# Attention and a bilinear FFN in one kernel: reciprocals of the softmax sums taken on 112 partitions, weights rounded in whole tiles and moved on ScalarE's DMA queue, q scaled and squared on ScalarE

## The chip, the cores and the metric

The kernel runs on one core of a Trainium2 chip. A core has five engines that work side by side, each through its own instructions in order: TensorE (PE, matmuls; its weight loads are PEld), VectorE (DVE), ScalarE (ACT), GpSimd (POOL) and SyncE (SP, which here only issues DMAs). The metric is the time of one execution on the device in microseconds (us), median of several.

## The reference

Weights arrive as float64, all else as float32. Cut to what matters:

```python
batch, n_heads, seq, head_dim = (8, 12, 448, 64)
q_n, k_n = (rmsnorm(q, g_q), rmsnorm(k, g_k))        # x / sqrt(mean(x*x) + 1e-6) * g
scores = np.matmul(q_n, k_n.transpose(0, 1, 3, 2)) / np.sqrt(head_dim)
attn = np.exp(scores - np.max(scores, axis=-1, keepdims=True))
attn = attn / (np.sum(attn, axis=-1, keepdims=True) + 1e-09)
x = np.matmul(attn, v)                               # heads side by side: (3584, 768)
out = ((x @ w_a) * (x @ w_b)) @ w_out                # w_a, w_b: (768, 1536), w_out: (1536, 768)
```

## The kernel before

**Attention.** Two heads make a pair; there are 48 pairs, six for each of the eight batch entries. For a pair, q and k are squared and summed by rows (L418 to L431), the reciprocal root comes from a power on POOL (L441), q is normalized (L445), both are transposed on PE (L474) and copied out of PSUM (`qkT`, L479 to L483). Scores `sc` (L496) come in four chunks of 112 keys; ACT takes the exponential (`ET`, L502, with k's norm as the scale); PE multiplies by v (`o`, L517) and by ones (`su`, L552), which gives each query's sum over keys, the same number on 64 partitions for each head. For the first 12 pairs (`LEAD`) `su` adds the four `ET` chunks on PE itself; later, DVE and POOL add them first (L530, L532). DVE inverts the sums (L570, two RECIPROCALs of 128x224) and multiplies the output by them (L591). In the lead the sums are copied out of PSUM by ACT first (L564) into `sum`, of which there is one buffer; later the RECIPROCAL works in PSUM, in the one buffer `su`.

**Weights.** A float64 weight is rounded to float32 from its two 32-bit words in seven elementwise steps (L260 on ACT, L261 to L267 on DVE, the last add L269 on POOL). Each of the 18 weight tiles comes as two halves of 128x768 that are loaded and rounded apart; four steps (L365, one of them on POOL) then form the further factors that a seven-product (Strassen-like) matrix product needs; the result `st` (7 x 384 columns, three buffers) is stored to DRAM (`kept`) for later use. All DMAs are issued by SP. Words wait in the space of `hT` (`hraw`, the first six weight tiles) and of `fin` (`lraw`).

**FFN.** Two batch entries at a time (`beta` 0 to 3). `quarter_products` makes 12 groups of seven products (`pq`, L741), `last_product` seven products for each of a few row blocks (`po`, L669). Products use two PSUM banks in turn, so DVE and ACT must empty one (L763 to L797) before the product after next. DVE also forms sums of operands (L605, L657).

**Order.** Every operation is entered in `Plan` with an engine, an assumed time, a key, its reads, writes and buffers. `Plan.run` plays the program forward: of the operations that could start soonest on an engine it takes the one with the smallest key. The order of each engine's instructions is what this play gives, and it is fixed when the kernel is built; at run time each engine goes through its list and waits where data are late. Three stretches follow from it: the **lead** (pairs 0 to 11, with the first weight tiles; about 19 to 177 us), the **rounding stage** (FFN of `beta` 0 beside pairs 12 and on, with the rest of the weights; to about 450 us), and the **late stage**.

Of the kernel before, what the change touches and what calls it, by code (L numbers as in the profile page):

```python
# [9 lines left out]
FP32 = mybir.dt.float32  # L10
# [15 lines left out]
class Plan:  # L26
# [6 lines left out]

    TURN = 0.18

# [7 lines left out]
    def op(self, engine, us, key, emit, reads=(), writes=(), new=(), mode=None, chain=None, kb=0):  # L43
# [19 lines left out]
        self.ops.append((engine, us, key, emit, deps, mode, chain, kb, tuple(new), tiles))  # L63
        return n

    def run(self):
# [18 lines left out]
        opened, free, modes, cands, dma = {}, {}, {}, {}, 0.0  # L85
# [25 lines left out]
        while any(cands.values()):  # L111
            best = None
            for e, cs in cands.items():
                f = free.get(e, 0.0) if e else 0.0
                at = {}
                for n in cs:
                    t = buffers(n)
                    if t is not None:
                        turn = self.TURN if ops[n][5] != modes.get(e) else 0.0
                        at[n] = max(f, ready[n], t) + turn  # L120
# [7 lines left out]
            for x in members(n):  # L128
# [14 lines left out]
                for u in users.get(x, ()):  # L143
                    ready[u] = max(ready[u], end[x])
# [15 lines left out]
def kernel(  # L160
# [39 lines left out]
    P = 128  # L200
# [42 lines left out]

    def round_steps(get):
# [7 lines left out]
        def step(do):  # L252
# [16 lines left out]
            ("POOL", 2, step(lambda hi, hif, lo, lof, w, wb: nc.gpsimd.tensor_tensor(w, w, lof, ALU.add)), "x", "w"))  # L269
# [18 lines left out]
    def fast_body(ld, wk, ps_s, ps_o, ps_mm, dram):  # L288
        plan = Plan()
        op, tile_of = plan.op, plan.tile  # L290
        NORM = 4.0
        LEAD = 12

# [5 lines left out]
        def rounding(key, size, get, x, w):  # L299

            for e, n, emit, r, wr in round_steps(get):
                rate = {"ACT": 950, "DVE": 1900 if n == 1 else 950, "POOL": 420}[e]
                op(e, 0.17 + size / rate, key, emit, [{"x": x, "w": w}[c] for c in r], [{"x": x, "w": w}[c] for c in wr])
# [6 lines left out]
        SLOTS, MORE = KO * 2 * S // NW, LATE // NW  # L310
# [5 lines left out]
        op(None, 0.0, -9, open_words, [], [f"{hraw}/{x}" for x in range(SLOTS)] + [f"{lraw}/{x}" for x in range(MORE)],  # L316
           new=[hraw, lraw])

        def place(early):
# [7 lines left out]
            return (lambda: hold[x][:, at * NW:(at + 1) * NW]), f"{name}/{at}"  # L327

        def factors(n, key, early, after):
# [10 lines left out]
            else:  # L340
                m, ab = order[n]
                src = (moe_w_a, moe_w_b)[ab]
                steps = ((0, 4, 3, 2), (1, 5, 0, 3), (0, 3, 4, 0), (0, 6, 1, 3))
            for part, quarters in enumerate((((0, 0), (0, 1)), ((1, 1), (1, 0)))):
                words, row = place(early)

                def load(words=words, quarters=quarters, part=part):
                    if last:
                        k = m + part * MH
                        nc.sync.dma_start(words(), moe_w_out[k * P:(k + 1) * P, :])  # L350
                        return
                    for x, (i, j) in enumerate(quarters):
                        nc.sync.dma_start(
# [632 lines left out]
```

## Time and profile before

| | us |
|---|---|
| median of 3 runs | 1692.31 (1691.57 to 1692.49) |
| the profiled execution | 1693.48 |
| its span, first to last instruction | 1692.0 |
| DVE busy | 891.9 |
| POOL busy | 571.1 |
| ACT busy | 365.9 |

The profile gives for each engine its busy time, a timeline, groups of instructions by source line with their mean duration, and waits: which engine stood idle before which instruction and what ended that. A name such as `pq<-x,st` says what is written and what is read; L741 is a line of the kernel. One float32 matmul of the program stands in the trace as two PE instructions. "PEclk" is the share of its clock that PE was granted.

### The profile page before, as it was taken

To read this page: it belongs to the slowest core of one execution; us is meant where nothing else is said; L and a number is where in the kernel's file an instruction comes from. 1 tells how busy PE (TensorE), PEld (TensorE's weight loads), DVE (VectorE), ACT (ScalarE), POOL (GpSimd) and SP (SyncE) were. 2 spreads that over 40 slices of the span, in tenths; PEclk is the share of its full clock that TensorE was granted. 3 is DMA by queue.
4 is the path that set the end of the run, shared out by engine and by line. 5 is a ranking of instruction groups with operands and counts; after the bars stand their busy time and mean duration, and the time that the engine had idled before them with its cause. 6 is when DMAs were issued, how large, how long until landed. Compare 5 with 4: busy or idle time off the path is not lost.

```text
span 1692.0 us, 14761 instructions
## 1 busy us (share of the span) xinstructions
PE 1606.0 (95%) x5448; PEld 774.1 (46%) x5448; DVE 891.9 (53%) x1094; ACT 365.9 (22%) x654; POOL 571.1 (34%) x326
## 2 busy tenths in 40 slices
PE   5989889988999999999999999999999999999998
PEld 2333334443444444455444544455544455555554
DVE  8996688999766645422265754522236722212331
ACT  5666233211222233200123123200012200000000
POOL 5454456564354444510054355410133200110000
PEclk9999899999999999999999999999999999999999
DMA  6664134444423332321222333222222242222131
GB/s 210 200 200 144 33 119 146 137 170 159 165 83 99 115 123 66 98 98 66 91 81 71 94 98 110 87 98 77 87 72 67 76 168 80 83 98 82 64 112 49
DMA packets 114294, 180.77 MB, mean 107 GB/s; under 512 B 50468, under 2 KB 102948, under 8 KB 104484
## 3 DMA queue, kind: packets, MB, share of 16 engines
q1 hardware_dynamic: 114212, 179.73, 32.0%
q8 instruction: 45, 0.74, 0.2%
q14 instruction: 37, 0.30, 0.1%
HBM read 143.92 MB, written 35.78 MB: 106 GB/s over the span
## 4 chain that ended last, share of the span: by engine, by line
PE 72%; DVE 20%; issue 3%; POOL 3%; DMA 1%; ACT 0%; SPq 0%; DVEq 0%; POOLq 0%; ACTq 0%
PE pq L741 37%; PE po L669 18%; PE sc L496 7%; PE o L517 6%; PE su L552 2%; DVE fin L657 2%; DVE st L261 2%; DVE st L262 2%; DVE st L264 2%; PE pt L474 1%; DVE su L570 1%; DVE sum L570 1%; DVE ms L431 1%; DVE st L365 1%; DVE lraw L267 1%
## 5 line engine op out<-in xcount | busy, mean ns | idle before, releaser
L741 PE MATMUL pq<-x,st 128*128 128x448 f32 x2016 | 780.8, 547 | 29.0 <-DVE U L769 8.6
L741 PEld LDWEIGHTS pq<-x,st 128*128 128x128 f32 x2016 | 383.1, 192 | 414.2 <-issue 373.5
L502 ACT ACTIVATE ET<-sc,ms 112x448 f32<-112x448 f32 x384 | 213.6, 637 | 352.5 <-PE sc L496 334.8
L669 PE MATMUL po<-st,hT 128*128 128x384 f32 x744 | 246.2, 487 | 0.0
L496 PE MATMUL sc<-qkT 64*112 64x448 f32 x768 | 178.4, 582 | 30.3 <-DVE qkT L483 19.5
L669 PEld LDWEIGHTS po<-st,hT 128*128 128x128 f32 x744 | 139.9, 190 | 100.6 <-issue 7.8
L570 DVE RECIPROCAL su<-su 128x224 f32<-128x224 f32 x72 | 112.7, 1565 | 116.9 <-PE su L552 115.8
L517 PE MATMUL o<-ET,v_sb 112*64 112x448 f32 x768 | 169.4, 564 | 3.0 <-ACT x L587 3.0
L532 POOL TENSOR_TENSOR sum<-sum,ET 112x896 f32<-112x896 f32 x72 | 158.8, 2205 | 35.1 <-DVE sum L530 34.1
L441 POOL TENSOR_TENSOR ms<-ms,expo 112x16 f32<-112x16 f32 x48 | 148.3, 3089 | 55.0 <-DVE ms L437 53.4
L788 POOL TENSOR_TENSOR hT<-hT,t 128x448 f32<-128x448 f32 x24 | 28.3, 1180 | 409.6 <-DVE t L787 409.6
L426 POOL TENSOR_TENSOR sq<-k_sb 112x512 f32<-112x512 f32 x36 | 49.4, 1372 | 330.1 <-DMA k_sb<-in_k_dram 205.7
L669 PE MATMUL po<-st,fin 128*128 128x384 f32 x432 | 145.3, 489 | 0.0
L496 PEld LDWEIGHTS sc<-qkT 64*112 64x112 f32 x768 | 62.2, 177 | 126.0 <-issue 68.2
L669 PEld LDWEIGHTS po<-st,fin 128*128 128x128 f32 x432 | 80.6, 190 | 61.2 <-issue 8.8
L517 PEld LDWEIGHTS o<-ET,v_sb 112*64 112x64 f32 x768 | 51.3, 141 | 110.7 <-issue 103.9
L689 DVE TENSOR_TENSOR o_sb<-fin,po 128x384 f32<-128x384 f32 x56 | 31.0, 553 | 110.9 <-PE po L669 110.4
L799 POOL TENSOR_TENSOR hT<-hT,t 128x448 f32<-128x448 f32 x48 | 58.8, 1228 | 61.8 <-DVE t L797 55.5
L763 ACT COPY hT<-pq 128x448 f32<-128x448 f32 x24 | 12.8, 532 | 290.5 <-PE pq L741 290.5
L431 DVE TENSOR_REDUCE ms<-sq 112x8 f32<-112x512 f32 x96 | 65.2, 679 | 13.6 <-POOL sq L426 13.5
L269 POOL TENSOR_TENSOR st<-st,lraw 128x768 f32<-128x768 f32 x24 | 47.5, 1978 | 66.7 <-DVE lraw L267 60.7
L797 DVE TENSOR_TENSOR t<-U,pq 128x448 f32<-128x448 f32 x48 | 29.7, 619 | 67.3 <-PE pq L741 67.3
(70 smaller groups left out, 1120.8 us busy)
## 6 DMA issues: line engine op xcount, KB each, us to landing
st<-kept SPq DMA_DIRECT2D x36, 1344.0 KB, 5.9
st<-kept_o SPq DMA_DIRECT2D x28, 1152.0 KB, 5.2
kept<-st SPq DMA_DIRECT2D x12, 1344.0 KB, 4.6
q_sb<-in_q_dram SPq DMA_DIRECT2D x48, 224.0 KB, 2.8
k_sb<-in_k_dram SPq DMA_DIRECT2D x96, 112.0 KB, 3.0
v_sb<-in_v_dram SPq DMA_DIRECT2D x48, 224.0 KB, 2.6
kept_o<-st SPq DMA_DIRECT2D x6, 1344.0 KB, 6.0
lraw<-in_moe_w_b_dram SPq DMA_DIRECT2D x20, 384.0 KB, 3.5
```

The costliest lines, as they stand in the source:

```text
L269: ("POOL", 2, step(lambda hi, hif, lo, lof, w, wb: nc.gpsimd.tensor_tensor(w, w, lof, ALU.add)), "x", "w"))
L426: nc.gpsimd.tensor_tensor(t, flat, flat, ALU.mult)
L431: nc.vector.tensor_reduce(rs[p][:, s], xs["sq", nm, p], AX, ALU.add)
L441: nc.gpsimd.tensor_tensor(msf, msf, expo, ALU.pow)
L496: nc.tensor.matmul(t[:, e, 0:S], lhsT=qkTs[p][rows, 1, c * SP:(c + 1) * SP], rhs=qkTs[p][rows, 0, :], start=True, stop=True)
L502: nc.scalar.activation(E[:, e], scs[p, c][:, e, 0:S], AF.Exp, scale=rs[p][:, 1, 2 * c + e:2 * c + e + 1])
L517: nc.tensor.matmul(os_[p][e * D:(e + 1) * D, :], lhsT=xs["v", p][:, e, c * D:(c + 1) * D], rhs=ETs[p, c][:, e], start=(c == 0), stop=(c == ...
L532: nc.gpsimd.tensor_tensor(sums[p], sums[p], ETs[p, c], ALU.add)
L570: op("DVE", 1.55, p, lambda half=half: nc.vector.reciprocal(sus[p][:, half], sus[p][:, half]), [], [su])
L669: nc.tensor.matmul(held["po"][:, 0:HALF], lhsT=a[0]()[:, c], rhs=sts[beta, 12 + place_of[f]][:, c], start=(c == 0), stop=(c == MH - 1))
L741: nc.tensor.matmul(banks[bank][:, 0:S], lhsT=sts[at][:, f, c * P:(c + 1) * P], rhs=quads[x][:, c], start=(start and c == 0), stop=(stop an ...
L799: take("POOL", 1.15, lambda i=i, n=n, nm=nm: nc.gpsimd.tensor_tensor(C(i, n), C(i, n), held[nm], ALU.mult), [t], [hp[i]])
```

## The change

- **Sums over keys.** In 44 of the 48 pairs ACT copies the sums out of PSUM (`rec`, three buffers). SP's DMAs spread one row for each head over 56 partitions (`few`, 112x8 for both heads), DVE inverts that, a DMA stores it to DRAM (`inv`), and two DMAs bring it back to 64 partitions each. The last pair of each `beta` (p = 11, 23, 35, 47) is inverted in PSUM as before.
- **Weights.** Each weight tile is rounded as a whole (128x1536), in its seven steps; the last add and all four factor steps are on DVE. Loads and the store to `kept` are issued by ACT.
- **q.** The scale on the way out of PSUM, and the squares of q and k, are on ACT for all pairs.
- **The play.** It counts 0.1 us more where a result goes to another engine (`LAG`), two DMA queues, and lets no operation marked `lock` (of DVE or POOL) start while another one runs. Parts of a quad `x` are tracked one by one. `GATES` and `seq` let eight weight tiles (not six) use the early space.

PE, after the lead. `pt` are transposes, `sc`, `o`, `su` the attention products, `pq` those of the FFN. Before:

```order
L474 MATMUL pt<-ident,k_sb 128x112 x4
L474 MATMUL pt<-ident,qn 128x112 x4
L741 MATMUL pq<-x,st 128x448 x12
L496 MATMUL sc<-qkT 112x448 x4
L517 MATMUL o<-ET,v_sb 64x448 x4
L741 MATMUL pq<-x,st 128x448 x3
L496 MATMUL sc<-qkT 112x448 x4
L552 MATMUL su<-sum,ones 64x448 x2
L517 MATMUL o<-ET,v_sb 64x448 x4
```

The same pair (p = 14) in the changed kernel:

```order
L488 MATMUL pt<-ident,k_sb 128x112 x4
L488 MATMUL pt<-ident,qn 128x112 x4
L776 MATMUL pq<-x,st 128x448 x3
L508 MATMUL sc<-qkT 112x448 x4
L529 MATMUL o<-ET,v_sb 64x448 x4
L776 MATMUL pq<-x,st 128x448 x3
L508 MATMUL sc<-qkT 112x448 x4
L564 MATMUL su<-sum,ones 64x448 x2
L529 MATMUL o<-ET,v_sb 64x448 x4
```

Between two parts of a pair there now stands one FFN product (x3) where there were up to four; most of what is taken out here stands later, as 189 `pq` in one piece.

DVE in the lead, around the reciprocal of a pair (`sum` before, `few` after). Before:

```order
L267 SCALAR_TENSOR_TENSOR hraw<-hraw 128x768
L570 RECIPROCAL sum<-sum 128x224 x2
L365 TENSOR_TENSOR st<-st 128x384 x3
L591 TENSOR_TENSOR x<-x,sum 128x448
L431 TENSOR_REDUCE ms<-sq 112x8
L570 RECIPROCAL sum<-sum 128x224
```

And in the changed kernel:

```order
L600 RECIPROCAL few<-few 112x8
L271 TENSOR_SCALAR st<-st 128x1536
L272 TENSOR_SCALAR st<-st 128x1536
L444 TENSOR_REDUCE ms<-sq 112x8
L451 TENSOR_SCALAR ms<-ms 112x16
L274 SCALAR_TENSOR_TENSOR st<-hraw,st 128x1536
L276 TENSOR_SCALAR hraw<-st 128x1536
L277 SCALAR_TENSOR_TENSOR hraw<-hraw 128x1536
L459 TENSOR_TENSOR qn<-q_sb,ms 112x2x4x64
L626 TENSOR_TENSOR x<-x,rec 128x448
L279 TENSOR_TENSOR st<-st,hraw 128x1536
```

The multiplication by the reciprocal (L626) stands nine rows behind it, and the last add of the rounding (L279) is now a DVE row.

ACT in the lead of the changed kernel, where it issues a load of weights and the store of the weight tile before (before, no DMA stood on ACT):

```order
L495 ACTIVATE qkT<-pt,gain 128x448
L514 ACTIVATE ET<-sc,ms 112x448 x2
L368 DMA hraw<-in_moe_w_b_dram 128x6x256 x2
L386 DMA kept_o<-st 896x1x384
L514 ACTIVATE ET<-sc,ms 112x448 x2
L437 ACTIVATE sq<-k_sb 112x512
L514 ACTIVATE ET<-sc,ms 112x448 x2
L437 ACTIVATE sq<-q_sb 112x512
```

The store waits for DVE's last factor step, and exponentials stand behind it.

The diff, cut to its core:

```diff
-                        at[n] = max(f, ready[n], t) + turn
+                        at[n] = max(f, ready[n], t, port if ops[n][10] else 0.0) + turn
...
+                if ops[x][10]:
+                    port = max(port, t)
                 if ops[x][7]:
-                    dma = max(dma, t) + ops[x][7] / 250.0
-                    end[x] = dma + 2.5
+
+                    dma[e] = max(dma[e], t) + ops[x][7] / (200.0 if dma["SP" if e == "ACT" else "ACT"] > t else 250.0)
+                    end[x] = dma[e] + 2.5
+                    if e == "SP":
+                        dma["ACT"] = max(dma["ACT"], t) + ops[x][7] / 300.0
...
                 for u in users.get(x, ()):
-                    ready[u] = max(ready[u], end[x])
+                    ready[u] = max(ready[u], end[x] + (self.LAG if ops[u][0] != e else 0.0))
...
-            ("POOL", 2, step(lambda hi, hif, lo, lof, w, wb: nc.gpsimd.tensor_tensor(w, w, lof, ALU.add)), "x", "w"))
+            (ROUND, 2, step(lambda hi, hif, lo, lof, w, wb: two[ROUND].tensor_tensor(w, w, lof, ALU.add)), "x", "w"))
...
-        SLOTS, MORE = KO * 2 * S // NW, LATE // NW
+        SLOTS, MORE = KO * 2 * S // (2 * NW), LATE // (2 * NW)
...
+            words, row = place(early)
+
+            for part in range(2):
+                def load(part=part):
+                    to = words()[:, part * NW:(part + 1) * NW]
...
-            parts = [0, 0, 2, 2, 4, 5, 6]
+                        nc.scalar.dma_start(to, moe_w_out[k * P:(k + 1) * P, :])
+                    else:
+                        at = part * HM + m * P
+                        nc.scalar.dma_start(to.rearrange("p (k n) -> p k n", k=KA),
+                                            src[:, 2 * at:2 * (at + P)].rearrange("(k p) n -> p k n", p=P))
+                op("ACT", 0.45, key - 2.5, load, after, [f"{row}/{part}"], kb=768)
...
+                e = FACTOR if pool_ else "DVE"
+                op(e, 1.05 if e == "POOL" else 0.6, key,
...
-            op("SP", 0.5, key, keep, [f"{st}/{x}" for x in range(7)], [f"kept{n}"], kb=1376)
+                    nc.scalar.dma_start(kept[n], sts[n].rearrange("p a b -> p (a b)"))
+            op("ACT", 0.45, key, keep, [f"{st}/{x}" for x in range(7)], [f"kept{n}"], kb=1376)
...
-                op("ACT" if p < LEAD else "POOL", 0.65 if p < LEAD else 1.05, key, square, [f"{nm}{p}"], [sq], new=[sq])
+                e = "ACT" if p < LEAD else SQUARE
+                op(e, {"ACT": 0.65, "POOL": 1.05, "DVE": 0.7}[e], key, square, [f"{nm}{p}"], [sq], new=[sq], lock=e != "ACT")
...
-                    elif p < LEAD:
+                    else:
                         nc.scalar.activation(qkTs[p][:, 0], pts[p, 0][:, 0:S], AF.Copy, scale=gain[:, 0:1])
-                    else:
-                        nc.vector.tensor_scalar_mul(qkTs[p][:, 0], pts[p, 0][:, 0:S], gain[:, 0:1])
...
             if c == 1:
-                op("DVE", 1.12, p, emit, [f"E{p}.0", f"E{p}.1", "moved"], [t], new=[t])
+                op("DVE", 1.12, p, emit, [f"E{p}.0", f"E{p}.1"], [t], new=[t], lock=True)
             else:
-                op("POOL", 2.1, p, emit, [f"E{p}.{c}"], [t])
+                op(ADD_UP, 2.1 if ADD_UP == "POOL" else 1.12, p, emit, [f"E{p}.{c}"], [t], lock=True)
...
+               [f"E{p}.{c}" for c in cs] if p < WIDE else [f"sum{p}"], [su], new=[su] if first else [], mode="cols", chain=chain)
             if not last:
                 return
-            if p < LEAD:
-
-                t = tile_of(f"sum{p}", "sum", 1)
-
-                def move():
-                    x = wk.tile([P, 2, S], FP32, tag="sum", name="sum")[:, 0]
-                    nc.scalar.copy(x, sus[p])
-                    sus[p] = x
-                op("ACT", 0.55, p - 0.5, move, [su], [t, "moved"], new=[t])
-                su = t
-            for x in range(2):
-                half = slice(x * S // 2, (x + 1) * S // 2)
-                op("DVE", 1.55, p, lambda half=half: nc.vector.reciprocal(sus[p][:, half], sus[p][:, half]), [], [su])
+            if p % (2 * HP) == 2 * HP - 1:
+
+                for x in range(2):
+                    half = slice(x * S // 2, (x + 1) * S // 2)
+                    op("DVE", 1.55, p, lambda half=half: nc.vector.reciprocal(sus[p][:, half], sus[p][:, half]), [], [su])
+                return
+
+
+            t, few = tile_of(f"rec{p}", "rec", 3), tile_of(f"few{p}", "few", 3)
+            fews = {}
+
+            def move():
+                x = wk.tile([P, S], FP32, tag="rec", name="rec", bufs=3)
+                nc.scalar.copy(x, sus[p])
+                sus[p] = x
+
+            def spread_out():
+                fews[0] = wk.tile([2 * FEW, S // FEW], FP32, tag="few", name="few", bufs=3)
+                for e in range(2):
+                    nc.sync.dma_start(fews[0][e * FEW:(e + 1) * FEW], sus[p][e * D:e * D + 1, :].rearrange("o (p i) -> o p i", p=FEW))
+
+            def leave():
+                fews[1] = dram.tile([2, S], FP32, name=f"inv{p}")
+                nc.sync.dma_start(fews[1].rearrange("e (p i) -> (e p) i", p=FEW), fews[0])
+
+            def come_back():
+                for e in range(2):
+                    nc.sync.dma_start(sus[p][e * D:(e + 1) * D, :], fews[1][e:e + 1, :].to_broadcast([D, S]))
+            op("ACT", 0.55, p - 0.5, move, [su], [t], new=[t])
+            op("SP", 0.8, p - 3.0, spread_out, [t], [few], new=[few], kb=20)
+            op("DVE", 0.25, p - 3.0, lambda: nc.vector.reciprocal(fews[0], fews[0]), [], [few])
+            op("SP", 0.4, p - 3.0, leave, [few], [f"inv{p}"], kb=20)
+            op("SP", 0.8, p - 3.0, come_back, [f"inv{p}"], [t], kb=230)
...
-            op("ACT", 0.55, p, take, [f"o{p}"], [x], new=[x] if c == 0 else [])
-            op("DVE", 0.75, p, divide, [f"sum{p}" if p < LEAD else f"su{p}"], [x])
+            op("ACT", 0.55, p, take, [f"o{p}"], [f"{x}/{c}"] + (["quarter"] if c == 0 else []), new=[x] if c == 0 else [])
+            op("DVE", 0.65, p, divide, [f"su{p}" if p % (2 * HP) == 2 * HP - 1 else f"rec{p}"], [f"{x}/{c}"], lock=True)
...
-        seq = [12, 13, 14, 0, 1, 2, 3, 4, 15, 5, 6, 16, 7, 8, 9, 17, 10, 11]
+        GATES = [0, 0, 1, 2, 3, 5, 7, 9, 10] + [12] * 9
+        seq = [12, 13, 14, 15, 16, 0, 1, 2, 3, 4, 5, 6, 7, 17, 8, 9, 10, 11]
...
-                    factors(n, x * 1.1 + 0.5, x < 6, [f"scored{p - 1}"] if p else [])
+                    factors(n, x * 1.1 + 0.5, x < 8, [f"scored{p - 1}"] if p else [])
```

More of the change, by code (lines that the diff above doesn't have):

```diff
@@ L34 @@
     TURN = 0.18
+    LAG = 0.1
     def __init__(self):
@@ L62, in op @@
         deps.discard(n)
-        self.ops.append((engine, us, key, emit, deps, mode, chain, kb, tuple(new), tiles))
+        self.ops.append((engine, us, key, emit, deps, mode, chain, kb, tuple(new), tiles, lock))
         return n
@@ L342, in factors @@
                 src = (moe_w_a, moe_w_b)[ab]
[L343 to L347, printed above, removed]
+                steps = ((0, 4, 2, 3), (1, 5, 0, 2), (0, 2, 4, 0), (0, 6, 1, 2))
+            words, row = place(early)
+            for part in range(2):
+                def load(part=part):
+                    to = words()[:, part * NW:(part + 1) * NW]
```

84 lines of the change are left out of this document (41 added, 43 removed).

## The prediction, made before the changed kernel was run

> **What bounds the kernel now.** The page comes first. Below: the span with the number of instructions, then busy times.
>
> ```profile
> span 1692.0 us, 14761 instructions
> ...
> PE 1606.0 (95%) x5448; PEld 774.1 (46%) x5448; DVE 891.9 (53%) x1094; ACT 365.9 (22%) x654; POOL 571.1 (34%) x326
> ```
>
> PE is the bound on the whole: it stands idle for 1692.0 - 1606.0 = 86 us. No edit removes a matmul, so what can be won is idle time, and time at a lower clock. The view by stretches tells where. Its columns: stretch, length, then busy time (instructions) of PE, PEld, DVE, ACT, POOL, then PE's granted clock, DMA share and GB/s. The stretches are start, lead, rounding stage, late stage and end.
>
> ```profile
> 0.00:18.80 18.80, 2.01 (x10) 1.34 (x10) 11.85 (x19) 7.77 (x11) 7.41 (x11) 1.00 0.75 246
> 18.80:177.00 158.20, 142.71 (x710) 54.23 (x710) 133.27 (x162) 98.83 (x182) 79.43 (x38) 0.98 0.56 175
> 177.00:450.00 273.00, 241.07 (x729) 108.79 (x730) 234.68 (x277) 63.71 (x105) 151.83 (x86) 0.94 0.38 132
> 450.00:1650.00 1200.00, 1184.66 (x3893) 589.20 (x3893) 504.70 (x625) 195.61 (x357) 332.41 (x192) 0.99 0.28 92
> 1650.00:1692.00 42.00, 35.51 (x111) 20.58 (x109) 7.40 (x14) 0.00 (x0) 0.00 (x0) 0.95 0.17 49
> ```
>
> Idle PE: 16.8, 15.5, 31.9, 15.3 and 6.5 us. Time lost to the clock (length times one minus the clock): lead 0.02 x 158 = 3.2, rounding stage 0.06 x 273 = 16.4; the late stage's 0.99 is too coarse, I take 6. So lead 18.7, rounding stage 48.3, late stage 21.3 us can be won at most. In lead and rounding stage DVE is busy for 84% and 86%. The waits name it (waiter, releaser: sum in us, times, longest):
>
> ```profile
> PE sc L496 <- DVE qkT L483: 19.5, 11, 3.4
> PE pq L741 <- DVE U L769: 8.6, 4, 2.4
> PE sc L496 <- ACT qkT L481: 7.7, 4, 3.2
> ```
>
> What holds DVE is seen in the timeline (start, length, instruction). First a wait of the lead that seems to be ACT's:
>
> ```profile
> 122.46 2.96 DVE L570 RECIPROCAL sum<-sum 128x224 f32<-128x224 f32 x2
> 125.33 1.89 DVE L365 TENSOR_TENSOR st<-st 128x384 f32<-128x384 f32 x3
> 127.14 0.62 DVE L591 TENSOR_TENSOR x<-x,sum 128x448 f32<-128x448 f32 x1
> 127.79 0.53 ACT L564 COPY sum<-su 128x448 f32<-128x448 f32 x1 [2.95 <-DVE x L591]
> 128.22 0.54 ACT L587 COPY x<-o 128x448 f32<-128x448 f32 x1
> 128.81 1.72 PE L517 MATMUL o<-ET,v_sb 112*64 112x448 f32 x8 [3.00 <-ACT x L587]
> ```
>
> ACT's copy of the next sums waits 2.95 us for the one buffer `sum`, which DVE holds through reciprocal and multiplication; PE then waits 3.00 us for the copy behind it. Then the rounding stage:
>
> ```profile
> 338.30 2.02 POOL L269 TENSOR_TENSOR st<-st,lraw 128x768 f32<-128x768 f32 x1 [4.73 <-issue]
> 338.67 2.07 DVE L262 TENSOR_SCALAR st<-st 128x768 uint32<-128x768 uint32 x1
> 340.66 0.61 DVE L776 TENSOR_TENSOR hT<-hT,pq 128x448 f32<-128x448 f32 x1
> 341.32 5.33 PE L741 MATMUL pq<-x,st 128*128 128x448 f32 x7 [4.39 <-DVE hT L776]
> ```
>
> A step of the rounding takes 2.07 us beside POOL's add and ends with it; the emptying of a PSUM bank (L776) stands behind, and PE waits 4.39 us.
>
> **The change, part by part.** The groups (line, engine, shape, count, busy us, mean ns, idle before) price it:
>
> ```profile
> L741 PE MATMUL pq<-x,st 128*128 128x448 f32 x2016 | 780.8, 547 | 29.0 <-DVE U L769 8.6 <-DVE t L782 5.5 <-DVE hT L776 5.2
> L570 DVE RECIPROCAL su<-su 128x224 f32<-128x224 f32 x72 | 112.7, 1565 | 116.9 <-PE su L552 115.8
> L570 DVE RECIPROCAL sum<-sum 128x224 f32<-128x224 f32 x24 | 36.1, 1529 | 10.7 <-ACT sum L564 10.6
> L437 DVE TENSOR_SCALAR ms<-ms 112x16 f32<-112x16 f32 x48 | 32.4, 675 | 1.2
> L483 DVE TENSOR_SCALAR qkT<-pt,gain 128x448 f32<-128x448 f32 x36 | 24.3, 676 | 0.0
> L266 DVE TENSOR_SCALAR lraw<-st 128x768 uint32<-128x768 uint32 x24 | 13.4, 560 | 0.6
> L262 DVE TENSOR_SCALAR st<-st 128x768 uint32<-128x768 uint32 x36 | 41.6, 1155 | 1.0
> L264 DVE SCALAR_TENSOR_TENSOR st<-hraw,st 128x768 uint32<-128x768 uint32 x12 | 11.4, 954 | 0.2
> L605 DVE TENSOR_TENSOR x<-x 128x1344 f32<-128x1344 f32 x16 | 24.9, 1555 | 0.3
> L365 DVE TENSOR_TENSOR st<-st 128x384 f32<-128x384 f32 x54 | 35.8, 663 | 7.7 <-POOL st L269 3.9 <-POOL st L365 2.5
> L269 POOL TENSOR_TENSOR st<-st,lraw 128x768 f32<-128x768 f32 x24 | 47.5, 1978 | 66.7 <-DVE lraw L267 60.7
> L426 POOL TENSOR_TENSOR sq<-k_sb 112x512 f32<-112x512 f32 x36 | 49.4, 1372 | 330.1 <-DMA k_sb<-in_k_dram 205.7
> L481 ACT ACTIVATE qkT<-pt,gain 128x448 f32<-128x448 f32 x12 | 7.9, 657 | 0.3 <-PE pt L474 0.3
> L424 ACT ACTIVATE sq<-k_sb 112x512 f32<-112x512 f32 x12 | 7.6, 632 | 23.6 <-DVE ms L431 23.6
> L564 ACT COPY sum<-su 128x448 f32<-128x448 f32 x12 | 6.5, 538 | 9.0 <-DVE x L591 5.6 <-PE su L552 3.4
> kept<-st SPq DMA_DIRECT2D x12, 1344.0 KB, 4.6
> q_sb<-in_q_dram SPq DMA_DIRECT2D x48, 224.0 KB, 2.8
> ```
>
> *Reciprocals.* 148.8 us of DVE go, less the 8 of the four pairs that stay (12.5). 44 small ones come. An instruction of 8 columns is not in the trace: between nothing and the 0.68 us of L437, which has 16; I take 0.2, as its work is a 28th of a RECIPROCAL of 224, so 9 us. Net -127. The chain ACT copy, DMA, DVE, DMA, DMA takes 0.54 + 0.2 + three landings; at 2.8 (q) that is 9 us, at 4.6 (kept) 15. What hides it: only the sums L605 need the multiplied output, and the last pair of each batch pair, on which they wait, skips the chain. A pair takes 158.2/12 = 13 us in the lead, so pair 10's chain just fits or is up to 2 us late, once in each of four `beta`. Behind SP's waits in the chain stand loads of q, k and v of later pairs, two buffers deep, 13 us a pair against a chain of 9 to 15: 0 to 2 us for each pair of the lead; I take 0, as it is nearer to the first.
>
> *Rounding.* Before, three TENSOR_SCALARs (0.56 each where unblocked, L266), two two-input steps (0.95, L264), for two halves, and three factor steps, at 0.55 when unblocked (by the row of 663 mean, at most 0.66): 2 x 3.58 + 1.7 = 8.9 us of DVE for a weight tile, 12 with the blocking in L262's mean. After: at twice the width a step takes between one and two of the halves; I take 1.7 times, so 2.9 and 3.2; the add on DVE 1.78 (L605 by width), four factor steps 2.2: 10.1 us. DVE's clean work so rises by 1.2 us for a tile (22 for 18), POOL's falls by 2 x 1.98 and a factor step.
>
> *POOL beside DVE.* 36 x 1.98 = 71 for the adds, 72 x 1.37 = 99 at most for the squares, so some 170 of POOL's 571 us go. L262 shows what they cost DVE: 1155 against 560, 0.6 us for each; with what remains on POOL I expect half of such blocking to stay.
>
> [...]
>
> *The play's new rules* act by the order alone. *ACT.* 36 x 0.657 + 72 x 0.632 + 32 x 0.538 = 86 us more, of which each late pair gets 2.5, on an engine that is busy for 195.6 of 1200 us there. In the lead it gets eight weight tiles (not six) and 24 DMA issues, and there it is busy for 62%. A load or store waits on DVE for data or space, and exponentials queue behind it on ACT, for which PE waits. How long is not in the trace. Bounds: 0, and the 2.95 us of the L564 row. There are 36 such places (18 pairs of loads, 18 stores). I take 0.3 us of PE each, 11 in all, near the lower end since the order puts them some rows behind the DVE row they need.
>
> *Sum.* Lead: DVE loses 11 reciprocals (34 us) and gets two tiles more (8 x 10.1 against 6 x 12, +9), so 108 of 158 us; the chain through `sum` explains three waits, of 3.0 and, by way of the copy of q, of up to 3.2; with their clock I take 8 of 18.7. Rounding stage: ten weight tiles (not twelve) are left for it, so DVE's work falls by 12 x 12 - 10 x 10.1 = 43 us, and by the reciprocals and q scales of six pairs (by PE's order; 6 x 3.8 = 23), from 235 to 169 us, 70% of what the stage would take; what stays is an emptying that finds a step of up to 1.8 us ahead of it. I take 32 of 48.3. Late: its 15.3 us of idle are nearly all waits for L483 (19.5 in the whole kernel); on ACT the scale stands behind a 0.54 us copy. I take 16 of 21.3 with the clock. ACT's DMAs give 11 back. Start and end: 0; q's loads now come first on SP, but ACT issues weight loads, some of which wait for landings, before it squares q (one landing of 2.8 either way). Together -8 - 32 - 16 + 11 = -45. The profiled execution took 1693.5, 1.2 more than the median of the runs: **1693.5 - 45 - 1.2 = 1647 us**.
>
> **The clock.** It is the term least sure:
>
> ```profile
> 308.70:312.10 3.40, 3.40 (x6) 1.50 (x5) 3.26 (x4) 1.84 (x3) 0.38 (x1) 0.50 0.91 298
> 443.70:447.10 3.40, 3.40 (x9) 1.81 (x10) 1.42 (x3) 0.53 (x1) 1.83 (x2) 1.00 0.00 0
> ```
>
> The first stretch follows a wait of 2.20 us and has half the clock, the second one of 2.37 us and has all of it. So waits over 2 us cost up to 1.7 us more, but not each.
>
> [...]
>
> **Rivals.** *DVE stays the bound of the rounding stage.* For a weight tile PE needs 780.8/48 = 16.3 us, DVE 10.1 + 5.5 emptyings at 0.61 = 13.5, 83%, in steps twice as long. If only 9 of the 48.3 us go: 1647 + 23 = 1670. For it: the stage's DVE share is so high; against: POOL is nearly out of it.
>
> *All waits of the three stretches go*, and ACT's DMAs cost nothing: 1692.3 - 18.7 - 48.3 - 21.3 = 1604; half way there, 1625.
>
> *Denser pairs wait as the lead does.* PE's order now has one product, not up to four, between the parts of a pair. The lead loses 18.7/12 = 1.6 us for a pair; for some 28 dense pairs that is 44 more: 1647 + 44 = 1691, no change. Against: two products, 12 x 0.387 = 4.6 us, still stand in each pair, and the lead's reason (`sum`) is gone.
>
> *Slower: ACT held by its DMAs.* Each of the 36 places costs PE 2.5 us (of the 2.95 bound) instead of 0.3: +79, 1726. From 1.5 us a place on (0.3 + 45/36) the kernel is slower than before. For it: ACT goes through its list in order, and so did the L564 wait reach PE in full. Against: DVE, on which it waits, has more air.
>
> **How the numbers follow.** Forecast 0.50 (1632 to 1660), DVE bound 0.20 (1660 to 1686), all waits gone 0.10 (1605 to 1632), no change 0.08, slower 0.12. A measurement of this kernel can tell about 0.2% (3.4 us) from no change; of the 0.08 a third falls on the faster side. Faster 0.50 + 0.20 + 0.10 + 0.03 = 0.83, same 0.05, slower 0.12. The range 1618 to 1690 leaves out half of the best case and the slower one, with a little of the no-change one: 0.2.
>
> **What would show it.** DVE busy near 892 - 127 - 24 + 22 = 763 us less half of the blocking, so 700 to 770; ACT near 450, POOL near 390. No PE wait on L483's successor above 1 us. In the rounding stage a clock of 0.97 or more, and PE waits on emptyings under 2 us. Wrong if PE waits for `ET` or `qkT` behind a DMA on ACT, or if `x` waits for `rec` at the sums.

## The result, and the profile after

| kernel | median us (lowest to highest) | ratio to before |
|---|---|---|
| before | 1691.96 (1691.57 to 1692.49) | 1 |
| changed | 1644.32 (1643.67 to 1645.44) | 0.9719, 95% interval 0.9702 to 0.9736 |

The changed kernel is 2.8% faster. Its profiled execution took 1645.44 us. First its page: the span, then the busy times of the engines.

```profile
span 1643.6 us, 14865 instructions
...
PE 1590.1 (97%) x5448; PEld 770.9 (47%) x5448; DVE 723.9 (44%) x960; ACT 432.5 (26%) x776; POOL 405.6 (25%) x200
```

The span is 48.4 us shorter. PE's idle time fell from 86 to 53.5 us, so by 32.5; the other 15.9 is PE's busy time. Most of that fits the clock: the mean granted clock over the span rose from 0.984 to 0.991, which is 12 us less lost to it. The view by stretches (columns as in the prediction; the late stage ends earlier now) says where:

```profile
0.00:18.80 18.80, 1.74 (x8) 1.33 (x8) 3.50 (x9) 3.49 (x6) 3.80 (x9) 1.00 0.82 240
18.80:177.00 158.20, 140.05 (x686) 52.47 (x686) 114.18 (x154) 103.95 (x182) 47.54 (x13) 0.95 0.68 218
177.00:450.00 273.00, 260.92 (x863) 119.80 (x860) 197.24 (x229) 89.00 (x148) 87.44 (x41) 0.98 0.39 135
450.00:1600.00 1150.00, 1150.00 (x3783) 575.62 (x3782) 401.64 (x555) 236.01 (x442) 266.86 (x138) 1.00 0.30 98
1600.00:1643.60 43.60, 37.38 (x116) 21.66 (x115) 7.40 (x14) 0.00 (x0) 0.00 (x0) 0.97 0.18 52
```

Idle time and loss by the clock together, counted as in the prediction: the lead has 18.2 + 0.05 x 158 = 26.1 us (before 18.7), the rounding stage 12.1 + 0.02 x 273 = 17.6 (before 48.3), the late stage nothing (before 21.3); start and end are as they were (17.1 and 6.2 of idle time, before 16.8 and 6.5). So **the lead lost 7 us, the rounding stage won 31 and the late stage 21**. PE's waits (waiter, releaser: sum, times, longest) no longer name DVE's q scale and the emptyings of banks first, but ACT:

```profile
PE sc L508 <- ACT ET L514: 11.2, 9, 4.4
PE pt L488 <- DVE qn L459: 10.3, 1, 10.3
PE sc L508 <- ACT qkT L495: 9.6, 6, 3.2
...
PE pq L776 <- DVE hT L814: 4.8, 1, 4.8
```

The two longest after the start are seen in the timeline. The one in the lead:

```profile
128.19 5.80 ACTq L368 DMA_DIRECT2D hraw<-in_moe_w_a_dram  x2
...
128.37 1.15 SPq L597 DMA_DIRECT2D rec<-inv  x2
...
134.04 1.16 ACT L514 ACTIVATE ET<-sc,ms 112x448 f32<-112x448 f32 x2 [6.20 <-DMA rec<-inv]
...
135.26 1.09 PE L508 MATMUL sc<-qkT 64*112 64x448 f32 x2 [4.38 <-ACT ET L514]
```

ACT issues the two loads of a weight tile. Between them it stands for most of 5.80 us, and it goes on when a DMA of SP, `rec<-inv`, has landed, with which the load shares no data; the wait of 6.20 us of ACT's next exponentials is put down to that landing. What ties the two was not shown. The exponentials stand behind the load, and PE waits 4.38 us. The one in the rounding stage:

```profile
283.15 2.07 POOL L544 TENSOR_TENSOR sum<-sum,ET 112x896 f32<-112x896 f32 x1
283.21 2.56 DVE L459 TENSOR_TENSOR qn<-q_sb,ms 112x512 f32<-112x512 f32 x1
...
286.87 1.13 SPq L597 DMA_DIRECT2D rec<-inv  x2
...
290.95 0.62 DVE L626 TENSOR_TENSOR x<-x,rec 128x448 f32<-128x448 f32 x1 [5.18 <-DMA rec<-inv]
...
291.49 0.61 DVE L814 TENSOR_TENSOR hT<-U,pq 128x448 f32<-128x448 f32 x1
292.16 1.12 PE L776 MATMUL pq<-x,st 128*128 128x448 f32 x1 [4.81 <-DVE hT L814]
```

DVE waits 5.18 us for a reciprocal that is still on its way: ACT's copy of these sums ended at 271.95, so the chain took 19.0 us. The emptying L814 stands behind the multiplication, and PE waits 4.81 us. The chain of DMAs has become a new wait in DVE's list.

The durations (groups of DVE; count, busy us, mean ns) are near those of the prediction: a step of the doubled rounding is 0.96 or 1.75 where unblocked, the small reciprocal 0.20.

```profile
L459 DVE TENSOR_TENSOR qn<-q_sb,ms 112x512 f32<-112x512 f32 x48 | 67.9, 1415 | 23.2 <-PE pt L488 11.2 <-POOL ms L455 7.3 <-issue 4.2
L626 DVE TENSOR_TENSOR x<-x,rec 128x448 f32<-128x448 f32 x44 | 28.7, 653 | 30.5 <-DMA rec<-inv 30.5
L279 DVE TENSOR_TENSOR st<-st,hraw 128x1536 f32<-128x1536 f32 x8 | 14.0, 1752 | 0.1
L600 DVE RECIPROCAL few<-few 112x8 f32<-112x8 f32 x44 | 8.8, 199 | 24.4 <-DMA few<-rec 24.1
L276 DVE TENSOR_SCALAR hraw<-st 128x1536 uint32<-128x1536 uint32 x8 | 7.7, 961 | 0.1
```

### The profile page after: what moved, and what is told of

Same layout as the page of the kernel before. It is cut to its first block, busy times and chain, and to the rows that moved or that the text cites. A ratio compares the mean times of both kernels' runs of the same rounds, so it can differ in the third digit from the quotient of the medians.

```text
span 1643.6 us, 14865 instructions
## 1 busy us (share of the span) xinstructions
PE 1590.1 (97%) x5448; PEld 770.9 (47%) x5448; DVE 723.9 (44%) x960; ACT 432.5 (26%) x776; POOL 405.6 (25%) x200
## 4 chain that ended last, share of the span: by engine, by line
PE 85%; DVE 5%; DMA 5%; ACT 1%; issue 1%; SPq 1%; POOL 1%; ACTq 0%; DVEq 0%; POOLq 0%
PE pq L776 44%; PE po L704 23%; PE sc L508 7%; PE o L529 7%; PE su L564 2%; PE pt L488 2%; DMA few<-rec 2%; DMA k_sb<-in_k_dram 2%; DMA inv<-few 1%; POOL ms L455 1%; DMA rec<-inv 1%; DVE ms L444 1%; DVE st L378 1%; SPq L418 0%; DVE x L640 0%
## 5 line engine op out<-in xcount | busy, mean ns | idle before, releaser
L776 PE MATMUL pq<-x,st 128*128 128x448 f32 x2016 | 769.7, 542 | 5.4 <-DVE hT L814 4.8
L455 POOL TENSOR_TENSOR ms<-ms,expo 112x16 f32<-112x16 f32 x48 | 152.2, 3171 | 241.1 <-DVE ms L451 219.2
L544 POOL TENSOR_TENSOR sum<-sum,ET 112x896 f32<-112x896 f32 x72 | 165.0, 2292 | 150.7 <-DVE sum L542 145.9
L459 DVE TENSOR_TENSOR qn<-q_sb,ms 112x512 f32<-112x512 f32 x48 | 67.9, 1415 | 23.2 <-PE pt L488 11.2
L542 DVE TENSOR_TENSOR sum<-ET 112x896 f32<-112x896 f32 x36 | 39.9, 1108 | 66.9 <-PE su L564 63.8
L829 DVE TENSOR_TENSOR hT<-U,pq 128x448 f32<-128x448 f32 x48 | 29.8, 621 | 74.5 <-PE pq L776 74.5
L801 ACT COPY t<-pq 128x448 f32<-128x448 f32 x24 | 12.8, 533 | 186.6 <-PE pq L776 186.6
```

The lines of the kernel that those rows point to most:

```text
L455: nc.gpsimd.tensor_tensor(msf, msf, expo, ALU.pow)
L459: nc.vector.tensor_tensor(qns[p].rearrange("p j h d -> p h j d"), xs["q", p].rearrange("p h (j d) -> p h j d", d=D), rs[p][:, 0].rearrange ...
L542: nc.vector.tensor_tensor(sums[p], ETs[p, 0], ETs[p, 1], ALU.add)
L544: two[ADD_UP].tensor_tensor(sums[p], sums[p], ETs[p, c], ALU.add)
L776: nc.tensor.matmul(banks[bank][:, 0:S], lhsT=sts[at][:, f, c * P:(c + 1) * P], rhs=quads[x][:, c], start=(start and c == 0), stop=(stop an ...
```

## The experiments

Each kernel ran in three rounds beside the kernel before. Differences between kernels are those of their ratios, times 1692 us.

### Parts of the change taken back one at a time

**Loads and stores issued by SP, in the changed kernel's order** (e1; so the four places):

```diff
-                        nc.scalar.dma_start(to, moe_w_out[k * P:(k + 1) * P, :])
+                        nc.sync.dma_start(to, moe_w_out[k * P:(k + 1) * P, :])
```

> The changed kernel with loads and stores of weights issued by SP at the same places of the order; ACT, DVE and PE keep their rows. Theory A (ACT's DMA instructions wait for landings of SP's DMAs and hold the exponentials behind them): the PE waits of 3.2 us (at 44.7) and 4.4 us (at 135.3) go, the first squares start near 7 us instead of 11.2, PE idle in the first 180 us falls from 37 to under 27 us, and the time is 1628 to 1638 us. Theory B (the lead waits for something else, such as q and k that come late because SP stands in the chain of the reciprocals): SP now has 54 DMAs more in front of q and k, PE idle there stays at 35 us or grows, and the time is 1644 to 1655.

1651.79 us, ratio 0.9761 (0.9745 to 0.9778): 7 us slower than the changed kernel. ACT is free of DMAs, the first transposes of q come at 14.94 us instead of 18.04, and yet PE waits longer. The timeline of e1 ahead of a wait of PE in the lead:

```profile
55.75 1.81 SPq L365 DMA_DIRECT2D hraw<-in_moe_w_out_dram  x2
...
57.73 1.16 SPq L593 DMA_DIRECT2D inv<-few  x1
...
65.95 1.15 SPq L597 DMA_DIRECT2D rec<-inv  x2
...
70.16 0.63 DVE L626 TENSOR_TENSOR x<-x,rec 128x448 f32<-128x448 f32 x1 [6.93 <-DMA rec<-inv]
...
73.55 0.63 DVE L444 TENSOR_REDUCE ms<-sq 112x8 f32<-112x512 f32 x1
73.66 0.33 SPq L593 DMA_DIRECT2D inv<-few  x1
...
74.22 0.63 ACT L437 ACTIVATE sq<-k_sb 112x512 f32<-112x512 f32 x1 [9.03 <-DVE ms L444]
...
75.95 1.09 PE L508 MATMUL sc<-qkT 64*112 64x448 f32 x2 [5.63 <-ACT ET L514]
75.97 0.61 SPq L597 DMA_DIRECT2D rec<-inv  x1
```

SP issues the store `inv<-few` right behind the two loads of a weight tile, and its return `rec<-inv` 8.2 us later; the next pair's, with no load ahead, comes after 2.3 us (73.66 to 75.97). DVE stands 6.93 us for that `rec`, the reduction behind it is late, ACT's square waits for the reduction, the exponentials stand behind the square, and PE waits 5.63 us. So DMAs that are moved but not planned for the queue they go to pass the hold on to the chain.

**All reciprocals on DVE** (e3): the four steps of the chain are replaced by

```diff
-            op("SP", 0.8, p - 3.0, spread_out, [t], [few], new=[few], kb=20)
...
+            for x in range(2):
+                half = slice(x * S // 2, (x + 1) * S // 2)
+                op("DVE", 1.55, p, lambda half=half: nc.vector.reciprocal(sus[p][:, half], sus[p][:, half]), [], [t])
```

> The changed kernel with the reciprocals of all pairs on DVE as two RECIPROCALs of 128x224 (on the copy rec, three buffers, for 44 pairs); no DMA chain. Theory A (the reciprocals on DVE were a main cost of before): DVE busy rises by 44 x 3.0 = 130 us to about 850, PE waits come back behind DVE in the rounding stage and the late stage, 1660 to 1675 us. Theory B (the one buffer sum and the work beside POOL were the cost, and not the length of the RECIPROCALs): 1636 to 1648, with a shorter lead since q and k no longer stand behind the chain on SP.

1640.21 us, ratio 0.9682 (0.9666 to 0.9699): 6 us **faster** than the changed kernel (the two intervals lie just apart), with DVE busy for 819.7 us instead of 723.9. The reduction of DVE's work on which most of the prediction is built, bought with the chain, brought nothing on balance here; what each of the two is worth alone this run does not tell. What is left of waits in this kernel shows the hold by a store, alone:

```profile
112.57 2.21 DVE L378 TENSOR_TENSOR st<-st 128x384 f32<-128x384 f32 x4
...
114.81 0.52 ACTq L386 DMA_DIRECT2D kept_o<-st  x1
115.37 0.53 ACT L493 COPY qkT<-pt 128x448 f32<-128x448 f32 x1 [2.56 <-DVE st L378]
...
116.49 1.09 PE L508 MATMUL sc<-qkT 64*112 64x448 f32 x2 [2.67 <-ACT qkT L495]
```

ACT stands 2.56 us at the store until DVE has written the last factor; the copies of the next pair's transposes stand behind it, and PE waits 2.67 us for them.

**The last add and a factor step on POOL** (e4) and **the q scale of the later pairs on DVE** (e6):

```diff
-    ROUND, FACTOR, SQUARE, ADD_UP, TIMES = "DVE", "DVE", "ACT", "POOL", "POOL"
+    ROUND, FACTOR, SQUARE, ADD_UP, TIMES = "POOL", "POOL", "ACT", "POOL", "POOL"
```

> The changed kernel with the last add of the rounding (128x1536) and one of the four factor steps back on POOL, still in whole tiles. Theory A (POOL's adds block DVE's steps beside them, and emptyings behind these, in the rounding stage): PE waits for emptyings of 2 to 4 us come back between 177 and 450 us, about a half of the 33 us won there is lost, 1655 to 1668 us. Theory B (the gain of that stage came from the reciprocals and from two weight tiles more in the lead): DVE is relieved by 42 us, 1640 to 1648.

```diff
-                    else:
+                    elif p < LEAD:
                         nc.scalar.activation(qkTs[p][:, 0], pts[p, 0][:, 0:S], AF.Copy, scale=gain[:, 0:1])
+                    else:
+                        nc.vector.tensor_scalar_mul(qkTs[p][:, 0], pts[p, 0][:, 0:S], gain[:, 0:1])
```

> The changed kernel with the scale of q on DVE for pairs 12 and on, as before. Theory A (the late stage's waits came from that copy standing behind sums on DVE): 10 to 15 us of PE waits for qkT come back after 450 us, with their clock 1655 to 1664 us. Theory B (they came from DVE's load with reciprocals and blocked sums, which is gone): under 5 us of such waits, 1644 to 1650.

1643.32 us (0.9709, 0.9693 to 0.9725) and 1646.46 us (0.9723, 0.9707 to 0.974): neither can be told from the changed kernel, and the late stage has no idle time in either. In e4 DVE's busy time falls by 9 us, to 715.3, and not by the 42 that were expected, as its steps grow with POOL busy for 493.5 us instead of 405.6: the mean of L271 from 1071 to 1265 ns, of L378 from 588 to 726, of L459 from 1415 to 1567. The time is the same even so. So neither of these two edits is needed by itself for what was won. Either the gain comes from elsewhere, or the edits stand in for each other.

### The order, and everything taken back at once

**The play without its new rules** (e7; `LAG = 0.0`, no lock) and **the kernel before with the new rules alone** (e8; `LAG = 0.1` and `lock=True` on the operations that have it in the changed kernel, no operation on another engine):

> The changed kernel whose play has neither the 0.1 us for a result that goes to another engine nor the lock between DVE and POOL; all placements stay. Theory P (the new rules of the play give most of the gain, as the order they make leaves room where a result changes engines): 1675 to 1692, and PE idle again for over 10 us between 450 and 1600 us, before sc and pq. Theory R (relief of DVE and POOL as a whole gives it, no single part being needed): 1640 to 1650, late stage without idle time as in the changed kernel.

> The kernel before, with the play's new rules alone (0.1 us for a result that goes to another engine; the lock between DVE and POOL), no operation placed elsewhere. Theory P: 1645 to 1665, late stage nearly without idle time of PE. Theory R: 1685 to 1700, since DVE is as busy as before (about 890 us).

e7: 1652.06 us, 0.9768 (0.9752 to 0.9785), 8 us lost. Its profiled execution is its fastest, 1645.98 against 1651.09 to 1653.65 of the others, so its trace does not show these 8 us. e8: 1681.09 us, 0.9936 (0.992 to 0.9953), 11 us won. So most of the gain is not the rules' own. But e8 shows what they do. Its rounding and late stages, and its waits:

```profile
177.00:450.00 273.00, 224.91 (x704) 102.73 (x705) 231.94 (x270) 63.33 (x103) 151.95 (x86) 0.91 0.37 128
450.00:1600.00 1150.00, 1150.00 (x3802) 570.74 (x3802) 463.38 (x614) 195.86 (x358) 319.20 (x192) 1.00 0.28 94
```

```profile
PE pq L744 <- DVE st L368: 28.2, 2, 16.4
PE pq L744 <- POOL st L272: 9.9, 1, 9.9
```

With nothing moved off DVE, **the late stage is without idle time**: here the new order alone does what the prediction gave to the scale on ACT. In exchange PE comes to the weight tiles too soon, and waits 38 us for `st`.

**Every placement taken back** (e9: e3, e4 and e6 together, squares of the later pairs on POOL, loads and stores on SP, issued and planned there). The play, the whole tiles, eight of them in the early space, and the copy of the sums of 44 pairs by ACT into three buffers stay:

> The changed kernel with every placement taken back at once: all reciprocals on DVE without the DMAs, last add of the rounding and factor steps on POOL, squares of the later pairs on POOL, q scale of the later pairs on DVE, loads and stores of weights on SP. The play, the whole tiles, eight tiles in the early space and three buffers for the copied sums stay. Theory P: 1640 to 1655. Theory R: 1675 to 1695, with DVE at 85% in the rounding stage and waits for the emptying of banks as before.

1661.09 us, 0.9816 (0.9798 to 0.9835): between the two theories, 20 us below e8. The waits for `st` are down to 6.9 us. In its late stage, though, PE waits 5.6 us for DVE's scale, in seven places: the new rules do not clear that stage in every kernel.

**Eight early tiles** (e14: the changed kernel with the gates and sequence of before):

```diff
-        GATES = [0, 0, 1, 2, 3, 5, 7, 9, 10] + [12] * 9
+        GATES = [0, 0, 1, 3, 5, 7, 8, 10, 11, 11] + [12] * 8
...
-                    factors(n, x * 1.1 + 0.5, x < 8, [f"scored{p - 1}"] if p else [])
+                    factors(n, x * 1.1 + 0.5, x < 6, [f"scored{p - 1}"] if p else [])
```

> The changed kernel with the gates and the sequence of weight tiles of before (six in the early space, not eight). Theory W (with the new play the products reach the weight tiles sooner, so with six of them early PE waits for the rounding; in the kernel before with the new play alone it waited 38 us for st in three places between 345 and 448 us): 1665 to 1685, with waits of pq for st. Rival (tiles are early enough since DVE has air): 1640 to 1650.

1658.42 us, 0.9798 (0.978 to 0.9816): 13 us lost, with 10.4 us of waits of `pq` for `st` in two places (the longest 6.96). Less than the theory's 21 or more, but of its kind: in the denser order, tiles 7 and 8 have to be ready early. The sequence of the tiles went back together with their number, so the two are not told apart.

### A kernel that beats both, and what it hangs on

**Reciprocals on DVE, loads and stores on SP** (e10: e3, with the DMAs issued by SP and planned there):

```diff
-                op("ACT", 0.45, key - 2.5, load, after, [f"{row}/{part}"], kb=768)
+                op("SP", 0.5, key - 2.5, load, after, [f"{row}/{part}"], kb=768)
...
-            op("ACT", 0.45, key, keep, [f"{st}/{x}" for x in range(7)], [f"kept{n}"], kb=1376)
+            op("SP", 0.5, key, keep, [f"{st}/{x}" for x in range(7)], [f"kept{n}"], kb=1376)
```

> The changed kernel with all reciprocals on DVE (no DMA chain) and loads and stores of weights on SP, planned there. Theory H (ACT is held in the lead and at the start by loads that wait for DMAs of SP; without any DMA on ACT and without the chain on SP nothing holds either): start 14.9 us to the first transposes instead of 18.0, lead's idle time 10 instead of 19, so 1628 to 1636. Rival (SP then holds q and k behind a load or store that waits, as in the run that only issued them from SP): 1640 to 1652.

**1622.91 us** (1622.12 to 1624.44), ratio 0.9596 (0.958 to 0.9612): 21 us below the changed kernel, below both expectations. Lead, rounding and late stage, then PE's waits in them:

```profile
18.80:177.00 158.20, 147.78 (x734) 57.30 (x730) 148.60 (x167) 108.87 (x191) 49.27 (x15) 0.97 0.65 208
177.00:450.00 273.00, 268.86 (x904) 123.97 (x904) 219.11 (x249) 95.47 (x158) 94.14 (x46) 1.00 0.39 134
450.00:1600.00 1150.00, 1150.00 (x3763) 579.29 (x3761) 434.47 (x570) 222.54 (x418) 242.43 (x130) 1.00 0.28 92
```

```profile
PE pt L488 <- DVE qn L459: 10.2, 3, 6.5
PE pt L488 <- DMA k_sb<-in_k_dram: 8.7, 1, 8.7
PE sc L508 <- ACT qkT L495: 5.8, 7, 1.2
```

DVE is busy for 94% of the lead, and PE waits there less than in either kernel: 10.4 us. After the start (8.74 and 6.50 us) no wait exceeds 2 us. As the play makes the whole order anew for the new places of the DMAs, the gain over e3 is that of both. From this kernel the three other placements were taken back singly (e11 by the line of e4, e12 by `SQUARE = "POOL"`, e13 by the lines of e6):

> The kernel with all reciprocals on DVE and loads and stores on SP (1623), with the last add of the rounding and one factor step of each weight tile on POOL as before. That kernel and the one with every placement taken back (1661) differ by this, by the squares and by the q scale: 38 us in all. Theory S (the steps beside POOL are what it hangs on): 1645 to 1661. Rival (the reciprocals' and the scale's place in DVE's list, not POOL): 1620 to 1630.

> The same kernel (1623) with the squares of q and k of the later 36 pairs on POOL. Theory S (POOL's work beside DVE): 1630 to 1645, with DVE's steps of the rounding longer by up to the length of a square (1.37). Rival: 1620 to 1630.

> The same kernel (1623) with the q scale of the later 36 pairs on DVE. By the prediction's reading of the waits for L483 (15.3 us of idle time in the late stage) this has a price of 10 to 20 us: 1633 to 1643, with waits of scores for DVE in the late stage. Rival (the waits for the scale were only the place where a late DVE showed): 1620 to 1628.

| | median us | ratio (95%) | lost to e10 |
|---|---|---|---|
| e11, add and a factor step on POOL | 1628.02 | 0.9621 (0.9605 to 0.9638) | 4 |
| e12, squares on POOL | 1635.44 | 0.9663 (0.9646 to 0.968) | 11 |
| e13, q scale on DVE | 1640.57 | 0.9695 (0.9678 to 0.9712) | 17 |

Together 32 of the 37 us between e10 and e9; e11's 4 us are at the edge of the noise, as its interval and that of e10 overlap. Here the q scale has a price, which it did not have in the changed kernel. DVE's timeline in e13 at the end of the lead, and the waits for it:

```profile
154.75 2.96 DVE L589 RECIPROCAL rec<-rec 128x224 f32<-128x224 f32 x2
...
158.88 1.54 DVE L589 RECIPROCAL rec<-rec 128x224 f32<-128x224 f32 x1
...
161.09 1.54 DVE L589 RECIPROCAL rec<-rec 128x224 f32<-128x224 f32 x1
...
163.80 0.67 DVE L497 TENSOR_SCALAR qkT<-pt,gain 128x448 f32<-128x448 f32 x1
```

```profile
PE sc L510 <- DVE qkT L497: 18.0, 10, 8.1
```

The first scale that DVE has to do stands behind the reciprocals of two pairs; the scores waited 8.1 us for it, at 164.62. It was not 15 us spread over the late stage, as the prediction had it: from 400 us on there are three waits of 1.5 to 1.9 us. e12's largest loss is at the same place, 7.49 us at 166.32, where PE waits for `qn`, and `qn` stands behind two reciprocals of 2.96 us together. They account for the last 1.7 us of that wait; until then the power on POOL, which `qn` needs too, was not done either.

In e6, without the long reciprocals, PE waits for the first scale at the same place:

```profile
175.60 0.20 DVE L602 RECIPROCAL few<-few 112x8 f32<-112x8 f32 x1 [6.44 <-DMA few<-rec]
...
176.88 0.68 DVE L497 TENSOR_SCALAR qkT<-pt,gain 128x448 f32<-128x448 f32 x1
177.61 1.84 PE L510 MATMUL sc<-qkT 64*112 64x448 f32 x4 [5.02 <-DVE qkT L497]
```

The scale now stands behind the small reciprocal, for which DVE waits 6.44 us until `few` has landed: the chain put a wait of its own where the long reciprocals had been. In all PE waits 7.5 us for the scale in e6, in three places, and none of it in the late stage; DVE stood idle before 29 of the 36 scales there, and before none in e13. That e6 takes no longer than the changed kernel comes in part from other waits, which happen to be shorter in its order: the 4.81 us for L814 are gone, and the longest for an emptying is 2.63.

So **with the reciprocals on DVE the scale costs 17 us; with the chain, no time that can be told from noise.** That both edits remove the same waits is likely for the late stage, but not true of the first scale, and e6 and e13 differ in the queue of the weight DMAs as well: no run changes the reciprocals alone beside a scale on DVE.

### The way from one kernel to the other

Each line is one of the kernels above, with one more group of edits:

| | ratio | step, us |
|---|---|---|
| before | 1 | |
| new rules of the play (e8) | 0.9936 | -11 |
| whole tiles, eight of them early, the sums of 44 pairs copied out by ACT into three buffers, parts of `x` tracked, other assumed times (e9) | 0.9816 | -20 |
| add and factor step on DVE, squares and q scale on ACT (e10) | 0.9596 | -37 |
| loads and stores on ACT (e3) | 0.9682 | +15 |
| reciprocals by DMA (the changed kernel) | 0.9719 | +6 |

The steps depend on the order in which they are taken, as e6 and e13 show. How the 20 us of e9 divide is known only for the eight tiles, 13 us by e14 in another surrounding; the rest was not tried apart.

## Why the prediction was right, and where it was not

**The sum.** 1647 was forecast, 1644.3 came. Three terms that erred make it up: the lead was to win 8 us and lost 7; the late stage won 21 instead of 16; and the 11 us for ACT's DMAs, which the prediction set apart, lie mostly in the lead, where -8 and +11 would be +3 against the +7 measured. The errors cancel, so that the total came out within 3 us is in part luck.

**DVE's and POOL's work.** Right: DVE 723.9 us (700 to 770 expected), ACT 432.5 (near 450), POOL 405.6 (near 390), the small reciprocal 0.20; a rounding step with one input took 0.961 / 0.562 = 1.71 times a half, one with two inputs 1.758 / 0.954 = 1.84 times (1.7 assumed for both). In the window of the rounding stage DVE was busy for 197.2 us and not 169, but that window now holds more of the FFN. That DVE's load sets the time, the base of the forecast, fell: with 96 us more on DVE, e3 is faster, and e10 is the fastest of all with DVE busy for 94% of the lead. In the waits shown here what counts is not how long DVE is busy but what stands ahead of the few operations for which PE waits.

**Rounding stage, -32.** Measured -31. The part given to fewer tiles in the stage is borne out in size by e14 (13 us), though not as the prediction put it: what PE waits for there is `st`, not an emptying behind DVE's steps. The part given to steps freed from POOL is not: with the add and a factor step back on POOL (e4) the time is the same, and in e11 they cost 4 us. An emptying under 2 us was expected; one waited 4.81, for a cause that was not in the sum, the multiplication's wait for `rec`.

**The chain of DMAs, hidden at no cost.** This step failed. "Only the sums L605 need the multiplied output" is true of the data, but the multiplication stands in DVE's list with others behind it. DVE stood 30.5 us before L626, by the group's row, and once an emptying stood behind. The chain's length was off as well: 9 to 15 us were assumed, and the one shown took 19.0. The price of the chain in the changed kernel, less what it relieved DVE of, is 6 us, by e3.

**Late stage, -16.** Right in size, wrong in cause. The scale on ACT was credited with it; e8 wins it with the scale on DVE and all reciprocals in place, by the order, and e6 has it too, with the scale on DVE. e7, with the old rules and all placements, has no idle time there either. So the placements together are enough, and in e8 so are the rules; whether the scale on ACT would be enough by itself was not tried.

**ACT's DMAs, 0.3 us at 36 places, at most 2.95.** The mechanism was right, and what the prediction named as a sign against itself came: PE waits for `ET` and `qkT` behind a DMA on ACT (4.38 and, at 44.69, 3.20 us; so the sign of no wait above 1 us on the scale's successor failed as well). The size was a mean over holds that are not alike: most places cost nothing, and the few that cost are longer than the upper bound, as ACT waits not only for DVE but, in the load at 128.19, for a landing on SP's queue (5.80 us). That bound came from a wait without a DMA in it. By e10 against e3 the DMAs on ACT cost 15 us, in kernels without the chain and with the order that follows from each; the chain beside DMAs planned on SP was not tried. The slower rival was thus real, but at a fifth of its price.

**Denser pairs** did not wait as the lead does: no wait of the late stage is left. And "all waits of the three stretches go" comes near only without two parts of the change, the chain and the DMAs on ACT: e10 comes to 1623, within that rival's 1605 to 1632.

**POOL beside DVE, and the second queue.** The moved add L279 took no longer than its width gives (1752 ns, 1.78 us assumed). Whether it is longer beside POOL was not seen: none of its 18 instances ran beside one of POOL's wide steps. `qn`, also a step with two inputs, did: at 283.21 it takes 2.56 us beside POOL's add L544 and ends 0.55 us after it. Of its 48 instances 33 ran beside L544, for 1.03 to 2.57 us each; the 15 others took 0.68 to 0.69. Together they take 67.9 us, 25 more than the 42.8 of the kernel before. PE waited for `qn` only at the start. On the second queue: with all DMAs on SP, e10 is 15 us faster than e3, so there a second queue brought no gain that outweighs the holds.

## What to carry to other kernels

An engine that works through a fixed list is judged by what stands ahead of the operations on the critical path, not by its busy share: 96 us less on VectorE, bought with a chain of DMAs, brought nothing, while moving 24 us of scales off it, the first of them from behind two pairs' reciprocals, brought 17. When a change has several parts that act on one engine's list, undo them singly and also all together, and build up from there: undone singly from the full change, the scale looked worthless, and in another surrounding it was worth 17 us. And read the trace of a run that came out the same, for its waits may have moved. A DMA put on a compute engine's queue brought its wait into that engine's list (5.80 us of ACT at 128.19; PE waited 4.38), so give such DMAs to an engine that has nothing else to do, and plan them there: e10 with them on SP came out 15 us below e3.

## What the runs showed of the hardware and the program

- A load issued by ACT waited for a DMA of SP's queue to land: 5.80 us between two loads at 128.19, and the 6.20 us that ACT's next operation waited are put down to `rec<-inv`. The load and that DMA share no data; what ties them was not shown.
- Half the clock followed PE gaps of 2.41 and 2.94 us in the changed kernel, and one of 2.20 in the kernel before. Two stretches of the changed kernel (columns as above, the granted clock is the third number from the end), the first behind a gap of 2.41 us, the second behind one of 2.94:

```profile
84.92:88.33 3.41, 3.41 (x12) 0.95 (x10) 2.56 (x5) 1.90 (x5) 0.00 (x0) 0.50 1.12 339
197.56:200.97 3.41, 3.41 (x5) 1.03 (x4) 3.09 (x3) 1.00 (x3) 3.33 (x3) 0.50 0.04 5
```

- The prediction left open why a wait of 2.20 us cost clock and one of 2.37 us did not. In the traces of these two kernels the starts of the stretches at half clock lie whole multiples of 3.41 us apart (13 starts before, 6 after). Measured between marks at that spacing, the 2.20 us before 308.36 lie in one interval of the kernel before (305.29 to 308.70); the 2.37 us before 443.69 are split by the mark at 441.82 into 0.50 and 1.87. After the start, 18 intervals at full clock held more than 2.0 us of PE idle time (13 before, 5 after, the last of each at PE's end), and half the clock followed each; it followed none with less than 1.4. In between both were seen: 1.84 us in the changed kernel with half the clock behind it, 1.99 in the kernel before without.
